# Three fp32r matmuls in place of one fp32 product in the FFT convolution of batches 2 to 8, with the rests taken by GpSimd

## The chip, the core and the metric

The kernel runs on one core of a Trainium2 chip. The metric is the device time of one execution in microseconds; the kernel before takes 2670.65 us (median of three runs, 2670.49 to 2672.26). All figures here are of that program and of one profiled execution of it.

## What is computed

Eight batches of a sequence of 3072 points with 256 channels go through a convolution by FFT and then through two dense layers:

```
X = np.fft.rfft(x, axis=1)
F = (filt_r + 1j * filt_i)[None, :, :]
y = np.fft.irfft(X * F, n=3072, axis=1)

h = np.maximum(np.maximum(x @ w1, x @ w2), x @ w3)      # 256 -> 768
x = h @ w_out                                           # 768 -> 256

h = x @ w_in                                            # 256 -> 1024
solu = h * softmax(h)
ln = (solu - mean) / sqrt(var + 1e-6) * g_ln
out = ln @ w_out                                        # 1024 -> 256
```

x is 8 x 3072 x 256 in float32. The program gets the weights as 64-bit floats and turns them to float32 itself.

## The kernel before

**Two stages.** In the first, some 1500 us, batch after batch goes through the convolution and the first dense layer ("MoE"), and its result is spilled to DRAM (lines 952 and 953). The second reads the spill and does the other layer (lines 1095 to 1200). It uses no part of what the change touches.

**Steps of the first stage.** The MoE is cut in 288 steps (b, tg, f): 8 batches, 6 tiles of 512 tokens, 6 slices of 128 of the hidden width. The text numbers them 0 to 287, so that batch b (counted from 0) begins with step 36 b and a tile with a multiple of 6. A step's `up` (line 920) is 12 matmuls of 512 columns; ScalarE, VectorE (DVE) and again both make `hm`, the maximum (925), `hh` and the rest `hl` (929). `down` (940 to 942) is 6 matmuls two steps later, with 12 more (949) at a tile's end. All operands there are split by hand in fp32r pairs, high part and rest, and each product is three matmuls: high by high, high by rest, rest by high. The PSUM pool of `h` has four banks, two steps' worth.

**The convolution.** A sequence of 3072 is 24 columns of 128 points. A chunk is one half (128 channels) of one batch, so chunk ch belongs to batch ch // 2. Chunks 0 and 1 (batch 0) are done ahead of the steps with a full complex DFT in `first_batch`. Chunks 2 to 15 are fed in by a generator, `fft_stream`, while the steps run. For each of four groups of columns a chunk does, in this order:

- `fwd_in`: twiddle factors on ScalarE and DVE into `U`, 6 x 128 columns for the three groups with `sl` other than 0;
- `middle`: two 128-point products `MA0`, `MA1` on TensorE (line 440); then `Z` (DVE, from PSUM), a swap of halves by two DMAs on SP's queue (515, 516), the filter in `M1` and `M2` (DVE), a difference on GpSimd, again a swap by DMA, and `EO` (DVE, two instructions);
- `inv_out`: two products `MB0`, `MB1` by `EO` (line 440), twiddle factors, and back into the chunk's slab `S`.

The group with `sl` 0 is treated apart and stays as it is. When both chunks of a batch are through, `inverse` combines the columns (DVE), and `flip` turns a tile for the MoE: two DVE transposes into `yt` (one for each chunk), 16 DMAs `zt<-yt` on SP's queue (line 880), then on ScalarE the cast `xh` and on DVE the rest `xl` (893, 894). The first `up` of a tile needs `xh` and `xl`. `yt` and `zt` have one buffer each.

**What sets the order.** The code after each step draws from `fft_stream` until DVE work worth 3200 ns is issued, or until 12 draws in a row brought none; `later()` makes a generator wait for the next step. The instructions so recorded are then put in order, engine by engine, by the framework's list scheduler, which goes by its own timeline and fixes each engine's queue; on the chip every engine works off its queue in that order. `have` would force convolution work out early if a tile's input were not recorded yet.

**Products.** `prod` (lines 437 to 440) is one fp32 matmul with the constant matrices `df` as stationary operand.

Of the kernel before, what the change touches and what calls it, by code (L numbers as in the profile page):

```python
# [11 lines left out]
F32R = mybir.dt.float32r  # L12
# [8 lines left out]
P = 128  # L21
# [124 lines left out]
def kernel(ctx: ExitStack, tc: tile.TileContext, x0, xr, ff, tw, dft, first_f, first_i,  # L146
# [135 lines left out]


    FULL = 2

    cost = [0.0]

# [146 lines left out]
    def rows(t, j0, j1):  # L434
        return t[:, j0:j1].rearrange("p s d -> p (s d)")

    def prod(o, mat, src, i0=None, i1=None, first=True, last=True):
        m = df[:, mat] if mat < 7 else dfull[:, mat - 7]
        v = src if i0 is None else rows(src, i0, i1)
        FZ['mm'] = nc.tensor.matmul(o, m, v, start=first, stop=last).ins  # L440

    def fwd_in(ch, g):
        sl, ks = GROUPS[g]
        X = S[ch]
        U = f2.tile([P, 8, P], F32, tag="U", name="U")
        n = len(ks)
        T = fc.tile([P, 6, P], F32, tag="T", name="T")
        if sl:
            for j, k in enumerate(ks):
                nc.scalar.activation(T[:, j:j + 4:3], X[:, sl:sl + 2, j], AF.Copy, scale=col("s", k))  # L450
                nc.scalar.activation(U[:, j:j + 4:3], X[:, sl:sl + 2, j], AF.Copy, scale=col("c", k))
            yield
            tt(U[:, 0:3], U[:, 0:3], T[:, 3:6], ALU.add)
            yield
            tt(U[:, 3:6], U[:, 3:6], T[:, 0:3], ALU.subtract)
            yield
        elif ch >= FULL:
            t, d = X[:, :, 1], X[:, :, 2]
            for j, k in enumerate((8, 20)):
                nc.scalar.activation(T[:, j], d[:, j], AF.Copy, scale=col("sh", k))  # L460
                nc.scalar.activation(U[:, j], t[:, j], AF.Copy, scale=col("c", k))
                nc.scalar.activation(T[:, 2 + j], d[:, j], AF.Copy, scale=col("ch", k))
                nc.scalar.activation(U[:, 2 + j], t[:, j], AF.Copy, scale=col("ns", k))
            yield
            tt(U[:, 0:4], U[:, 0:4], T[:, 0:4], ALU.add)
            yield
        else:
            t, d = X[:, :, 1], X[:, :, 2]
            nc.scalar.copy(U[:, 0], X[:, 0, 0])
            nc.scalar.activation(U[:, 1], X[:, 1, 0], AF.Copy, scale=col("c", 12))  # L470
            nc.scalar.activation(U[:, 5], X[:, 1, 0], AF.Copy, scale=col("ns", 12))
            nc.gpsimd.memset(U[:, 4], 0.0)
            yield
            for j, k in enumerate((8, 20)):
                nc.scalar.activation(T[:, j], d[:, j], AF.Copy, scale=col("sh", k))
                nc.scalar.activation(U[:, 2 + j], t[:, j], AF.Copy, scale=col("c", k))
                nc.scalar.activation(T[:, 2 + j], d[:, j], AF.Copy, scale=col("ch", k))
                nc.scalar.activation(U[:, 6 + j], t[:, j], AF.Copy, scale=col("ns", k))
            yield
            uu = U.rearrange("p (r s) d -> p r s d", r=2)[:, :, 2:4]  # L480
            tt(uu, uu, T[:, 0:4].rearrange("p (r s) d -> p r s d", r=2), ALU.add)
            yield
        ST["u", ch, g] = U
        yield
# [3 lines left out]
    def later():  # L488
        n = STEP[0]
        yield  # L490
        while STEP[0] == n and not NOW[0]:
            yield
# [6 lines left out]
    def middle(ch, g):  # L499
        dc = ch % 2  # L500
        sl, ks = GROUPS[g]
        n = len(ks)
        W = n * P
        real = g == 3 and ch >= FULL
        R = 2 * P if real else 0
        foff = sum(2 * P * len(GROUPS[i][1]) for i in range(4 if real else g))

        def pair(tag, name, pool=fc):
            t = pool.tile([P, 2, 4, P], F32, tag=tag, name=name)
            return t.rearrange("p r s d -> p (r s d)")[:, :2 * W].rearrange("p (r w) -> p r w", r=2)  # L510

        def swap(v):

            t = fc.tile([P, 512], F32, tag="swap", name="swap")[:, :v.free_size()]
            nc.sync.dma_start(t[64:], v[:64])
            nc.sync.dma_start(t[:64], v[64:])
            return t

        odd = ch < 2 and UNITS.index((ch, g)) % 2
        F = pair("Z" if odd else "F", "F")  # L520
        nc.sync.dma_start(F.rearrange("p r w -> p (r w)"), ff[dc, :, foff:foff + 2 * W])
        src = ST.pop(("u", ch, g))
        pf = pairbank(ch)
        if ch < FULL:
            for r, (mr, mi) in enumerate(((FRR, FIR), (FRI, FII))):
                prod(pf[:, r, :W], mr, src, 0, n, True, False)
                prod(pf[:, r, :W], mi, src, n, 2 * n, False, True)
                yield
            M1 = pair("EO", "Y", f2)
            M2 = pair("M2" if odd else "M1", "M2")  # L530
            tt(M1, pf[:, 0:1, :W].to_broadcast([P, 2, W]), F, ALU.mult)
            yield
            tt(M2, pf[:, 1:2, :W].to_broadcast([P, 2, W]), F, ALU.mult)
            yield
            tt(M1[:, 0], M1[:, 0], M2[:, 1], ALU.subtract)
            SUMS[ch, g] = tt(M1[:, 1], M1[:, 1], M2[:, 0], ALU.add).ins
            yield
            ST["y", ch, g] = M1
            yield
            return  # L540
        u = col("u", 0)
        if real:
            prod(pf[:, 0, 0:P], MO, S[ch][:, 1, 0])
            prod(pf[:, 0, P:R], MF0, S[ch][:, 0, 0])
            prod(pf[:, 0, R:W], MA0, src, 0, 2)
            yield
            prod(pf[:, 1, R:W], MA1, src, 2, 4)
            TAKEN.add(ch)
        else:
            prod(pf[:, 0, :W], MA0, src, 0, n)  # L550
            yield
            prod(pf[:, 1, :W], MA1, src, n, 2 * n)
        yield
        Z = pair("Z", "Z")
        M2 = pair("M2", "M2")
        nc.scalar.mul(M2[:, 0, R:], pf[:, 1, R:W], -1.0)
        nc.scalar.copy(M2[:, 1, R:], pf[:, 0, R:W])
        if real:
            nc.scalar.copy(Z[:, 0, :R], pf[:, 0, :R])
        stt(Z[:, :, R:], pf[:, :, R:W], u, M2[:, :, R:])  # L560
        ZS = swap(Z[:, 0])
        yield
        M1 = pair("M1", "M1")
        tt(M1[:, :, R:], Z[:, 1:2, R:].to_broadcast([P, 2, W - R]), F[:, :, R:], ALU.mult)
        if real:
            tt(M1[:, 0, :R], Z[:, 0, :R], F[:, 0, :R], ALU.mult)
        yield
        EO = pair("EO", "EO", f2)
        tt(M2[:, :, R:], ZS[:, R:].unsqueeze(1).to_broadcast([P, 2, W - R]), F[:, :, R:], ALU.mult)
        if real:  # L570
            stt(M2[:, 1, :R], ZS[:, :R], col("sg", 0), F[:, 1, :R], ALU.mult)
        yield
        tt(M1[:, 1, R:], M1[:, 1, R:], M2[:, 0, R:], ALU.subtract, nc.gpsimd)
        RS = swap(M1[:, 1, R:])
        tt(M1[:, 0, R:], M1[:, 0, R:], M2[:, 1, R:], ALU.add, nc.gpsimd)
        if real:
            tt(EO[:, 0, :R], M1[:, 0, :R], M2[:, 1, :R], ALU.add, nc.gpsimd)
        yield
        yield from later()
        with behind_step():  # L580
            stt(EO[:, 0, R:], RS, u, M1[:, 0, R:], ALU.subtract)
            stt(EO[:, 1, R:], M1[:, 0, R:], u, RS)
        yield
        ST["y", ch, g] = EO
        yield

    def inv_out(ch, g):
# [3 lines left out]
        io = 0 if sl else 1  # L591
        src = ST.pop(("y", ch, g))
        pf = pairbank(ch)
        src = src.rearrange("p r (s d) -> p (r s) d", d=P)
        if ch < FULL:
            prod(pf[:, 0, :W], IRR, src, 0, n, True, False)
            prod(pf[:, 0, :W], IIR, src, n, 2 * n, False, True)
            yield
            prod(pf[:, 1, io * P:W], IRI, src, io, n, True, False)
            prod(pf[:, 1, io * P:W], III, src, n + io, 2 * n, False, True)  # L600
        elif not sl:
            prod(pf[:, 0, :P], MOI, src, 0, 1)
            prod(pf[:, 0, P:W], MB0, src, 1, n)
            yield
            prod(pf[:, 1, 2 * P:W], MB1, src, n + 2, 2 * n)
        else:
            prod(pf[:, 0, :W], MB0, src, 0, n)
            yield
            prod(pf[:, 1, io * P:W], MB1, src, n + io, 2 * n)
        yield  # L610

        def zz(r, j):
# [146 lines left out]
    def first_batch():  # L759
# [53 lines left out]
        for i, u in enumerate(UNITS):  # L813
# [28 lines left out]
            if i == 7:  # L842
                turn_in(0, 0, *UNITS[6])
        GATE.append(behind)
        with tc.issue_after(FZ["mm"]), tc.issue_after(FZ["sent"].ins):
            for q in range(4):
                quarter(3, q, nc.scalar, xs[3, q])
# [477 lines left out]
```

## Time and profile before

| | |
|---|---|
| median of three runs | 2670.65 us |
| profiled execution, its own time | 2670.15 us |
| its span, first to last instruction | 2668.4 us |
| TensorE (PE) busy | 2648.6 us, 99% of the span |
| DVE, ScalarE (ACT), GpSimd (POOL) busy | 79%, 58%, 33% |
| line 440, PE busy | 210.5 us, all before 1340 us |
| last matmul of the first layer | about 1611 us |

The span is read by stage: what an engine has to do between 100 and 1340 us, with the convolution beside the MoE, differs from what follows. A matmul's own duration in the trace includes the time it takes to flow through the array; its price in a row of others is the distance from one start to the next. Records of one fp32 product come in pairs, so "x4" at line 440 is two products.

### The profile page before, as it was taken

What the parts mean: (1) busy time and instruction counts of PE and PEld (TensorE: products, weight loads), DVE (VectorE), ACT (ScalarE), POOL (GpSimd) and SP (SyncE); (2) the same over time, 40 slices, a digit from 0 to 9 for tenths busy, and PEclk for the clock granted to TensorE, in tenths of its full rate; (3) what the DMA queues carried; (4) which work ended last, traced back from release to release, by engine and by line L of the source; (5) the groups of instructions that cost most, each with busy time, mean ns of one, the idle gap of its engine ahead of it and who ended that gap; (6) DMA issues with size and microseconds to landing.
All of it is one profiled execution on the core that took longest, in us unless ns stands there. A gap on an engine that the chain in (4) does not pass through costs nothing.

```text
span 2668.4 us, 38588 instructions
## 1 busy us (share of the span) xinstructions
PE 2648.6 (99%) x12452; PEld 2183.5 (82%) x12452; DVE 2113.2 (79%) x3545; ACT 1559.9 (58%) x2960; POOL 892.9 (33%) x1311
## 2 busy tenths in 40 slices
PE   8999999999999999999999999999999999999999
PEld 5778888878877878888788888888888888888888
DVE  7796788987988988988785448878888878787875
ACT  5645554454454554554543336777777777777775
POOL 0011121011010010010110005666667676767675
PEclk9999999999999999999999999999999999999999
DMA  8534222224133242232222105555555555555553
GB/s 252 147 113 130 84 80 75 83 76 127 50 88 108 65 129 63 69 95 63 79 85 80 43 22 139 150 139 146 145 142 143 143 146 142 143 144 150 139 129 87
DMA packets 169063, 295.56 MB, mean 111 GB/s; under 512 B 33724, under 2 KB 101052, under 8 KB 167228
## 3 DMA queue, kind: packets, MB, share of 16 engines
q1 hardware_dynamic: 113848, 231.49, 32.4%
q10 hardware_dynamic: 53716, 56.89, 6.7%
q0 software_dynamic: 1296, 4.72, 0.6%
q8 instruction: 98, 1.61, 0.3%
q14 instruction: 105, 0.86, 0.1%
HBM read 97.40 MB, written 56.62 MB: 58 GB/s over the span
## 4 chain that ended last, share of the span: by engine, by line
PE 64%; DVE 2%; DMA 2%; SPq 1%; issue 1%; ACT 0%; POOL 0%; DVEq 0%; POOLq 0%; ACTq 0%
PE h L1111 20%; PE h L920 13%; PE p L1180 13%; PE p L1182 7%; PE o L941 2%; PE o L942 2%; PE o L940 2%; PE o L949 2%; PE pf L440 2%; SPq L880 1%; DMA swap<-M 0%; DMA swap<-Z 0%; DMA raw<-in_w_in_dram 0%; DMA raw<-in_w_out_dram 0%; DVE h L925 0%
## 5 line engine op out<-in xcount | busy, mean ns | idle before, releaser
L291 POOL TENSOR_TENSOR M<-M,M 128x384 f32<-128x384 f32 (+1 forms) x112 | 128.4, 1167 | 1093.0 <-DVE M L291 871.1
L1173 POOL TENSOR_TENSOR sl<-zt,sh 128x1024 fp32r<-128x1024 f32 x188 | 453.6, 2413 | 119.3 <-ACT sh L1172 96.7
L1180 PE MATMUL p<-V,sh 128*128 128x512 f32 x1536 | 380.4, 389 | 0.0
L928 ACT CAST hh<-h 128x512 fp32r<-128x512 f32 x288 | 169.2, 589 | 353.6 <-DVE h L925 344.5
L1122 DVE SCALAR_TENSOR_TENSOR sp<-h,e 128x1024 f32<-128x1024 f32 x192 | 234.0, 1219 | 152.6 <-ACT e L1120 150.6
L1180 PEld LDWEIGHTS p<-V,sh 128*128 128x128 f32 x1536 | 287.3, 188 | 59.3
L923 ACT ACTIVATE hm<-h 128x512 f32<-128x512 f32 x288 | 174.2, 606 | 183.5 <-PE h L920 179.0
L1120 ACT ACTIVATE e<-h,sm 128x1024 f32<-128x1024 f32 x192 | 213.8, 1114 | 110.1 <-DVE sm L1118 70.5
L1118 DVE TENSOR_REDUCE sm<-h 128x1 f32<-128x1024 f32 x192 | 231.5, 1206 | 47.0 <-PE h L1111 46.0
L1172 ACT CAST sh<-zt 128x1024 fp32r<-128x1024 f32 x188 | 196.6, 1047 | 106.6 <-PE p L1180 91.8
L1124 ACT ACTIVATE e<-sp,sm 128x1024 f32<-128x1024 f32 x192 | 220.5, 1148 | 54.2 <-DVE sm L1126 42.4
L1111 PE MATMUL h<-wih,x2h 128*128 128x512 f32 x768 | 243.1, 392 | 1.2 <-ACT xo L952 1.2
L1111 PE MATMUL h<-wih,x2l 128*128 128x512 f32 x768 | 242.0, 391 | 0.0
L925 DVE TENSOR_TENSOR h<-hm,h 128x512 f32<-128x512 f32 x288 | 196.9, 686 | 55.0 <-PE h L920 51.1
L1111 PE MATMUL h<-wil,x2h 128*128 128x512 f32 x768 | 238.3, 390 | 0.0
L1139 DVE STREAM_TRANSPOSE yt<-sp 128x1024 f32<-128x1024 f32 x188 | 231.4, 1231 | 5.3 <-DMA zt<-yt 1.5
L940 PE MATMUL o<-hh,woh 128*128 128x512 f32 x576 | 233.0, 404 | 0.0
L929 DVE TENSOR_TENSOR hl<-h,hh 128x512 fp32r<-128x512 f32 x288 | 196.0, 682 | 46.6 <-ACT hh L928 46.1
L941 PE MATMUL o<-hl,woh 128*128 128x512 f32 x576 | 228.0, 396 | 0.2 <-DVE hl L929 0.2
L942 PE MATMUL o<-hh,wol 128*128 128x512 f32 x576 | 225.8, 392 | 0.0
L1182 PEld LDWEIGHTS p<-V,sl 128*128 128x128 f32 x1536 | 209.7, 190 | 14.9
L1182 PE MATMUL p<-V,sl 128*128 128x256 f32 x1536 | 214.9, 282 | 0.0
(185 smaller groups left out, 5621.8 us busy)
## 6 DMA issues: line engine op xcount, KB each, us to landing
zt<-yt SPq DMA_DIRECT2D x752, 128.0 KB
x<-xo SPq DMA_DIRECT2D x96, 256.0 KB
x<-x ACTq DMA_DIRECT2D x48, 512.0 KB
F<-in_ff_dram SPq DMA_DIRECT2D x48, 384.0 KB
S<-in_xr_dram SPq DMA_DIRECT2D x12, 1536.0 KB
out_dram<-ob ACTq DMA_DIRECT2D x144, 128.0 KB
zt<-yt SPq DMA_DIRECT2D x560, 32.0 KB
F<-in_ff_dram SPq DMA_DIRECT2D x16, 512.0 KB
```

What stands on the lines that cost most here:

```text
L920: nc.tensor.matmul(ph[j], wt[:, c, f * P:(f + 1) * P], xt[:, c], start=i == 0, stop=i == 5)
L940: nc.tensor.matmul(po[m], wo_h[:, f, cs], hh, start=f == 0, stop=False)
L941: nc.tensor.matmul(po[m], wo_h[:, f, cs], hl, start=False, stop=False)
L942: nc.tensor.matmul(po[m], wo_l[:, f, cs], hh, start=False, stop=False)
L1111: nc.tensor.matmul(h[:, fs], xt[:, c, ts], wt[:, c, fs], start=n == 0, stop=n == 5)
L1118: nc.vector.tensor_reduce(sm[:, 0:1], h, axis=AX.X, op=ALU.max, negate=True)
L1122: nc.vector.scalar_tensor_tensor(sp, h, 1.0, e, op0=ALU.mult, op1=ALU.mult, accum_out=sm[:, 2:3])
L1124: nc.scalar.activation(e, sp, AF.Square, bias=sm[:, 3:4], accum_out=sm[:, 4:5])
L1139: nc.vector.transpose(out=YT[g][:, :, t].rearrange("p j c k -> p c j k"), in_=sp.rearrange("p (c j k) -> p c j k", c=NF2, j=4))
L1173: nc.gpsimd.tensor_tensor(lv, z, hv, op=ALU.subtract)
L1180: nc.tensor.matmul(p, sh[:, c], V2[:, c], start=c == 0, stop=False)
L1182: nc.tensor.matmul(p[:, :D], sl[:, c], V2[:, c, :D], start=False, stop=c == NF2 - 1)
```

## The change

Where a chunk is 2 to 15 and the group's `sl` is not 0, `U` and `EO` (128 x 768 each) are split before the products: ScalarE casts the high part to fp32r, GpSimd subtracts it for the rest. `prod` then makes three fp32r matmuls of 384 columns with the constants `dh` and `dl`, split once at the end of `first_batch` into the buffer of `dfull`. Both splits are followed by a `later()`. There are 14 chunks x 3 groups = 42 pairs of splits (84 casts, 84 subtractions) and 42 x 4 = 168 products, which become 504 matmuls. The four new tiles `Uh`, `Ul`, `EOh` and `EOl` take 3 KB a partition each, and the scratch of the software DMA queue is 4 KB a partition in place of 16. One product of `inv_out` is written in another way, with the same columns.

```
+    SPLIT = tuple(range(2, 16))
+    def split(v, tag):
+        hi, lo = (fc.tile([P, 6, P], F32R, tag=tag + s, name=tag + s) for s in "hl")
+        nc.scalar.copy(hi, v)
+        nc.gpsimd.tensor_tensor(lo, v, hi, op=ALU.subtract)
+        return hi, lo
...
     def prod(o, mat, src, i0=None, i1=None, first=True, last=True):
+        if isinstance(src, tuple):
+            hi, lo = (rows(v, i0, i1) for v in src)
+            dh, dl = FZ["dh"][:, mat], FZ["dl"][:, mat]
+            nc.tensor.matmul(o, dh, hi, start=True, stop=False)
+            nc.tensor.matmul(o, dl, hi, start=False, stop=False)
+            nc.tensor.matmul(o, dh, lo, start=False, stop=True)
+            return
...
+            if ch in SPLIT:
+                U = split(U[:, :6], "U")
+                yield
+                yield from later()
...
+        if sl and ch in SPLIT:
+            EO = split(EO.rearrange("p r (s d) -> p (r s) d", d=P), "EO")
+            yield
+            yield from later()
...
+        if SPLIT:
+            dd = fc.tile([P, 2, 4, P], F32R, tag="dfull", name="dd")
+            FZ["dh"], FZ["dl"] = dd[:, 0], dd[:, 1]
+            with tc.issue_after(FZ["sent"].ins):
+                nc.scalar.copy(FZ["dh"], df[:, 0:4])
+            nc.gpsimd.tensor_tensor(FZ["dl"], df[:, 0:4], FZ["dh"], op=ALU.subtract)
...
-    nc = bacc.Bacc("TRN2", target_bir_lowering=False, num_devices=1)
+    nc = bacc.Bacc("TRN2", target_bir_lowering=False, num_devices=1, dynamic_dma_scratch_size=4096)
```

The edit moves every later line by 8 to 30, so 440 becomes 449 to 451 (the three matmuls), 880 becomes 910, 920 becomes 950, 925 and 929 become 955 and 959. It also moves the instructions in the queues. Counted by the rows of line 929 (959) that stand ahead of it, the last product of chunk 15 stands in step 232 before and in step 246 after, and the second transpose of the first tile of batches 2 to 7 stands at steps 53, 101, 132, 168, 204 and 239 before, and at 59, 95, 134, 174, 214 and 249 after, where the tiles' first `up` is step 78 (their second tile, since the first goes another way), 108, 144, 180, 216 and 252.

**PE, step 200 before and step 216 after.** `pf` is a PSUM bank of a product, `EO` its moving operand (`EOh` and `EOl` the new pair), `dd` the new constants, `o` the sum of `down`.

```order
L920 MATMUL h_10859<-xl_10634,w0h_138 128x512 x2
L920 MATMUL h_10859<-xh_10633,w0l_140 128x512 x2
L440 MATMUL pf_10216<-EO_10093,df_136 128x384 x2
L941 MATMUL o_10792<-hl_10789,woh_145 128x512
L942 MATMUL o_10792<-hh_10788,wol_146 128x512
```

```order
L449 MATMUL pf_10877<-EOh_10823,dd_661 128x384
L450 MATMUL pf_10877<-EOh_10823,dd_661 128x384
L451 MATMUL pf_10877<-EOl_10824,dd_661 128x384
L449 MATMUL pf_11056<-Uh_10904,dd_661 128x384
L450 MATMUL pf_11056<-Uh_10904,dd_661 128x384
L451 MATMUL pf_11056<-Ul_10905,dd_661 128x384
L950 MATMUL h_12174<-xh_12091,w0h_138 128x512
L950 MATMUL h_12175<-xh_12091,w1h_139 128x512
```

Where two fp32 matmuls stood between those of a step, two times three stand now; at step 216 they come behind all of tile (5,5) and ahead of the first `up` of batch 6, whose two `h` banks then alternate.

**DVE, the transposes for the first tile of batch 6** (`yt`; `S` is a chunk's slab), before and then after.

```order
L929 TENSOR_TENSOR hl_10877<-h_10860,hh_10876 128x512
L925 TENSOR_TENSOR h_10887<-hm_10900,h_10887 128x512
L876 STREAM_TRANSPOSE yt_11275<-S_7601 128x4x4x32
L876 STREAM_TRANSPOSE yt_11275<-S_9246 128x4x4x32
L929 TENSOR_TENSOR hl_10904<-h_10887,hh_10903 128x512
```

```order
L303 SCALAR_TENSOR_TENSOR S_9777<-scr_10749 128x2x384 x2
L955 TENSOR_TENSOR h_12065<-hm_12078,h_12065 128x512
L906 STREAM_TRANSPOSE yt_11876<-S_9777 128x4x4x32
L955 TENSOR_TENSOR h_12106<-hm_12119,h_12106 128x512
L303 SCALAR_TENSOR_TENSOR Z_10889<-pf_10873,tws_135,M2_10890 128x768
L303 SCALAR_TENSOR_TENSOR EO_10751<-swap_10756,tws_135,M1_10680 128x384
L303 SCALAR_TENSOR_TENSOR EO_10751<-M1_10680,tws_135,swap_10756 128x384
L959 TENSOR_TENSOR hl_12082<-h_12065,hh_12081 128x512
L959 TENSOR_TENSOR hl_12123<-h_12106,hh_12122 128x512
L299 TENSOR_TENSOR M1_10908<-Z_10889,F_10871 128x768
L299 TENSOR_TENSOR M2_10890<-swap_10894,F_10871 128x768
```

The two transposes stood together in step 204; the second now follows the maximum of step 214 (`h_12065`), right behind the last instruction of `inverse`, and the maximum of step 215 (`h_12106`) follows it.

**SP, the 16 DMAs of that tile**, before and then after (`swap` are the swaps of halves, `F` a filter load).

```order
L880 DMA zt_11276<-yt_11275 32x256 x7
L515 DMA swap_10496<-Z_10490 64x512
L516 DMA swap_10496<-Z_10490 64x512
L880 DMA zt_11276<-yt_11275 32x256 x4
L515 DMA swap_10513<-M1_10506 64x256
L516 DMA swap_10513<-M1_10506 64x256
L521 DMA F_11108<-in_ff_dram 128x768
L880 DMA zt_11276<-yt_11275 32x256 x5
```

```order
L910 DMA zt_11877<-yt_11876 32x256 x4
L534 DMA swap_10894<-Z_10889 64x384
L535 DMA swap_10894<-Z_10889 64x384
L910 DMA zt_11877<-yt_11876 32x256 x4
L540 DMA F_11054<-in_ff_dram 128x768
L534 DMA swap_10942<-M1_10908 64x384
L535 DMA swap_10942<-M1_10908 64x384
L910 DMA zt_11877<-yt_11876 32x256 x8
```

Both orders have swaps among the 16; after, the last eight stand behind a swap of `M1_10908`, which is made from the `Z_10889` that follows the maximum of step 215.

## Rows read from the trace of the kernel before

**Rows 1.** The page's first part; 210 to 1110 us, busy by engine; a PE wait.

```profile
PE 2648.6 (99%) x12452; PEld 2183.5 (82%) x12452; DVE 2113.2 (79%) x3545; ACT 1559.9 (58%) x2960; POOL 892.9 (33%) x1311
...
210.00:1110.00 900.00, 899.46 (x3972) 725.40 (x3971) 776.00 (x1195) 463.40 (x1058) 100.72 (x90) 1.00 0.29 87
...
PE pf L440 <- DVE EO L295: 0.3, 1, 0.3
```

**Rows 2.** Timeline of PE, first stage: start, duration, line, operands, count.

```profile
705.51 1.45 PE L440 MATMUL pf<-U,df 128*128 128x384 f32 x4
706.50 0.92 PE L920 MATMUL h<-xh,w1h 128*128 128x512 f32 x2
707.26 0.63 PE L920 MATMUL h<-xl,w1h 128*128 128x512 f32 x2
```

**Rows 3.** Timeline of PE, second stage: eight matmuls of 512 columns, eight of 256.

```profile
2004.18 1.98 PE L1180 MATMUL p<-V,sh 128*128 128x512 f32 x8
2006.00 1.11 PE L1182 MATMUL p<-V,sl 128*128 128x256 f32 x8
2006.95 0.63 PE L1111 MATMUL h<-wih,x2h 128*128 128x512 f32 x2
```

**Rows 4.** Groups by tile: min/median/max ns, first and last start.

```profile
L619 ACT COPY v<-pf x12: 778/800/802, 34.4 to 238.7; 128x768 f32<-128x768 f32 x12
L1061 POOL TENSOR_TENSOR wil<-we,wih x4: 1289/1301/1317, 1371.9 to 1385.5; 128x512 fp32r<-128x512 f32 x4
L291 POOL TENSOR_TENSOR EO<-M,M x14: 722/740/1507, 180.6 to 1330.1; 128x256 f32<-128x256 f32 x14
```

**Rows 5.** Groups by line and shape: count, busy us, mean ns, idle before.

```profile
L295 DVE SCALAR_TENSOR_TENSOR Z<-pf,tws,M 128x768 f32<-128x768 f32 x42 | 42.3, 1008 | 9.2 <-ACT M L557 9.0
L291 DVE TENSOR_TENSOR M<-swap,F 128x768 f32<-128x768 f32 x42 | 39.8, 948 | 10.2 <-DMA swap<-Z 10.2
L295 DVE SCALAR_TENSOR_TENSOR EO<-M,tws,swap 128x384 f32<-128x384 f32 x42 | 25.6, 610 | 0.0
L929 DVE TENSOR_TENSOR hl<-h,hh 128x512 fp32r<-128x512 f32 x288 | 196.0, 682 | 46.6 <-ACT hh L928 46.1
L893 ACT CAST xh<-zt 128x512 fp32r<-128x512 f32 x70 | 40.8, 642 | 0.0
L876 DVE STREAM_TRANSPOSE yt<-S 128x512 f32<-128x512 f32 x70 | 45.6, 685 | 11.8 <-DMA zt<-yt 11.6 <-issue 0.2
L291 DVE TENSOR_TENSOR scr<-scr 128x384 f32<-128x384 f32 x46 | 27.0, 626 | 0.0
L291 DVE TENSOR_TENSOR S<-scr 128x768 f32<-128x768 f32 x34 | 31.8, 962 | 0.0
L295 DVE SCALAR_TENSOR_TENSOR S<-scr 128x768 f32<-128x768 f32 x46 | 41.6, 944 | 0.0
```

**Rows 6.** Timelines of SP's queue and DVE: a tile's 16 DMAs, a swap's two.

```profile
1417.82 11.17 SPq L880 DMA_DIRECT2D zt<-yt  x16
1430.40 1.31 DVE L876 STREAM_TRANSPOSE yt<-S 128x512 f32<-128x512 f32 x2 [4.92 <-DMA zt<-yt]
...
956.52 0.46 SPq L515 DMA_DIRECT2D swap<-M  x1
957.03 0.60 SPq L516 DMA_DIRECT2D swap<-M  x1
```

**Rows 7.** Timeline of PE, then windows of PE: length, busy, granted clock, DMA.

```profile
90.79 5.30 PE L865 MATMUL h<-im,z 96*128 96x96 f32 x24 [2.46 <-ACT S L796]
...
91.00:92.00 1.00, 1.00 (x6) 0.51 1.14 204
...
101.00:102.00 1.00, 1.00 (x5) 0.87 0.07 25
```

**Rows 8.** Timelines of DVE and GpSimd: one instruction, and two, that took long.

```profile
1103.06 1.77 DVE L295 SCALAR_TENSOR_TENSOR scr<-scr,S 128x768 f32<-128x768 f32 x1
...
910.84 4.32 POOL L291 TENSOR_TENSOR M<-M,M 128x384 f32<-128x384 f32 x2 [73.22 <-DVE M L291]
```

More of the change, by code (lines that the diff above doesn't have):

```diff
@@ L593, in inv_out @@
         pf = pairbank(ch)
-        src = src.rearrange("p r (s d) -> p (r s) d", d=P)
+        if not isinstance(src, tuple):
+            src = src.rearrange("p r (s d) -> p (r s) d", d=P)
         if ch < FULL:
@@ L608, in inv_out @@
             yield
-            prod(pf[:, 1, io * P:W], MB1, src, n + io, 2 * n)
+            prod(pf[:, 1, :W], MB1, src, n, 2 * n)
         yield
```

## The prediction

> **What bounds the kernel now.** I read the busy times first: TensorE is busy for 99% of the span, and in 210 to 1110 us, where the changed work lies, for 899.46 of 900 us, against 776 of DVE, 463 of ScalarE and 101 of GpSimd [rows 1]. The waits of PE come next: on the products' operand `EO` it waited once, 0.3 us [rows 1]. So TensorE's own work sets the time there, and a microsecond taken from it is won, as long as the operands still come in time. The third look is at prices of TensorE's work [rows 2, 3], the fourth at what must be done between a chunk's last columns and the next batch's first `up` [rows 5, 6], the fifth at the clock behind a wait [rows 7].
>
> **Part 1, the products: -21.5 us.** From 705.51 to 707.26 there are 1.75 us, in which two fp32 products of 384 columns and two fp32r matmuls of 512 start [rows 2]. Eight fp32r matmuls of 512 take 2006.00 - 2004.18 = 1.82, or 0.2275 each, and eight of 256 take 0.95, or 0.119 each [rows 3]. So a product costs (1.75 - 2 x 0.2275)/2 = 0.648. An fp32r matmul of 384 columns stands midway between 0.119 and 0.2275, at 0.173, and three cost 0.520. That is 0.128 less, and 168 x 0.128 = 21.5 us. Bounds: 0.16 for the matmul, in proportion to the columns alone, would be 28; with 0.19, if every change of weights costs a little more, it would be 13.
>
> **Part 2, the splits: nothing on ScalarE and GpSimd by their sums, but a latency.** A ScalarE copy of 128x768 takes 0.80 [rows 4], so 84 casts are 67 us over some 1100, on an engine that is half idle [rows 1]. A GpSimd subtraction takes 0.74 at 256 columns and 1.30 at 512 [rows 4]; along that line 768 cost 1.86, and 84 make 156 us, on an engine with 800 of 900 us free [rows 1]. If the other work were not there, each pair would cost TensorE its 2.7 us; it is there, since `later()` puts the products behind the next step, which is 18 matmuls of 0.2275, 4.1 us. What remains is that a product's operand comes 2.7 us later, in a queue that had 0.3 us of waits. I take 3.0 us for waits on `U` and `EO` outside the two places of part 4, between 0 and 6: the lower end is what the 0.3 of [rows 1] says, the upper a wait of 2 us at three of the 84 splits, and I take the middle.
>
> **Part 3, constants and scratch: +0.6 us.** The high part of the constants is a cast of 512 columns, 0.64 by the row of `xh` [rows 5], at the end of `first_batch`, where ScalarE's copies of `S` are already what TensorE waits for [rows 7]. I count it whole, 0.6 (0 to 1.3, the upper end if the subtraction is waited for too). The subtraction, 1.30 [rows 4], stands on GpSimd between weight DMAs and is needed by the first split product, many steps later. The smaller scratch I put at nothing: the software queue moves 1296 packets in all in the profiled execution, nine DMAs' worth, none of them beside the steps that count here. If it did bind, one weight would come later in the first 100 us.
>
> **Part 4, the end of a batch: +14.2 us.** Here the gain can go. The `later()`s make chunks end later. The second transpose for batch 6 moves from step 204 to 214, with the first `up` at 216; that for batch 7 from 239 to 249, with the first `up` at 252. Before, 12 steps, some 50 us, lay between; now one or two. I add up step 216 in the order of the rows on SP and DVE that the section on the change shows, from the end of the `up` of step 215, t = 0. The maximum of 215 ends at about 1.1 (0.7 as its like `hl`, and some 0.4 before it starts). Then `Z` 1.01, to 2.1; two `EO` of 0.61, to 3.3; two `hl` of 0.68, to 4.6; `M1` and `M2`, 0.95 each, to 6.5 [rows 5]. GpSimd's difference of 384 columns takes 1.0 on the line of part 2, to 7.5. The swap's two DMAs hold SP for 0.46 and 0.60 [rows 6], to 8.5. Only then come the last eight of the 16 `zt` DMAs, 0.70 each (16 in 11.17 [rows 6]), to 14.1. Landing takes 1430.40 - 1417.82 - 11.17 = 1.4 [rows 6], to 15.5, and the cast `xh` 0.64 [rows 5], to 16.2.
>
> Against this TensorE has, ahead of that `up`, the 18 `down` matmuls of the steps left and the tile's 12 more, 30 x 0.2275 = 6.8, and 12 matmuls of 384, 2.1; in between it waits for `EOh` (`EO` at 3.3, cast to 4.1, while TensorE is there after 13 matmuls at 3.0), 1.2. It is through at 10.1 and stands for 6.1, which with the 1.2 is **7.3 us** (3 if the DMAs are already issued ahead of the swap on the chip, 10 if DVE is behind by a chunk).
>
> For step 252, from the end of the `up` of 249: DVE still has the last combinations, 2 x 0.63 + 2 x 0.96 + 0.68 + 2 x 0.94 = 5.7 [rows 5], less what is done by then; I put the maximum of 249 at 4.2 and the transpose at 4.9. All 16 DMAs follow, 11.2, to 16.1; with landing and cast the operand is there at 18.1. TensorE has 72 matmuls, 16.4. It waits **1.8 us** (0 to 5).
>
> **The clock.** At 90.79 TensorE had waited 2.46 us; from 91 on the granted clock is 0.51 of 2.4 GHz, the lower level of 1.2, and between 101 and 102 it is back on average at 0.87 [rows 7]. So some 10.2 us were run at half speed, and 5.1 lost. The wait at 216 is longer than that one, so I add **5.1 us** once; the 1.8 at 252 is shorter, and I add none. Sum of the part: 7.3 + 5.1 + 1.8 = 14.2.
>
> **Sum.** -21.5 + 3.0 + 0.6 + 14.2 = -3.7 us on the profiled execution's 2670.15: 2666.45. The median of the runs is 0.5 above that execution, so 2667.0. A difference of 0.2%, 5.3 us, is about what can be told from no change: faster is below 2665.3, slower above 2676.0.
>
> **Rivals.**
>
> *No wait at the batches' ends: 2653.* If DVE and SP reach the transposes and DMAs of step 216 earlier against TensorE than my sum has it, only parts 1 to 3 are left: 2670.65 - 21.5 + 3.6 = 2652.8; with a wait shorter than the 2.46 of the row, which leaves the clock up, as much as 2655, and with half the part-2 waits too, 2651. For it: the order before has the same pattern (the `up` of two steps alternating behind a finished tile) at four other steps (30, 36, 54 and 60, within 210 to 1110 us), and the 900 us hold 0.54 us of idle time in all [rows 1]. Against it: the sum needs 6 us to be wrong by. Chance 0.28.
>
> *The clock falls three times: 2678.* The wait at 252 reaches 2.5 us (0.7 more than I have), the clock falls there too (5.1), and one of the waits of part 2 also reaches 2.5 (5.1): -3.7 + 0.7 + 10.2 = +7.2, so 2677.9. Its place is TensorE in front of the first `up` of batch 7 and in front of a product by `EOh`. It turns into slower only with the third fall. For it: the price of a wait is more than its length [rows 7], and 18.1 against 16.4 is a close race. Against it: ordinary products have 2.7 us of new latency in 4.1 of cover. Chance 0.20.
>
> *GpSimd holds up DVE: 2673.* In the trace a DVE instruction of 768 columns with two operands took 1.77 where its like takes 0.95, and a pair of GpSimd subtractions of 384 took 4.32 in place of 2.0 [rows 5, 8]: when both run, one stands. The change adds some 62 GpSimd subtractions of 1.86 us in 210 to 1110 (84 over about 1220 us). If each kept DVE for its whole length, it would be 62 x 1.86 = 115 us of DVE; the 900 us, less the 15.9 that TensorE would win there (62/84 of 21.5), leave 884.1 - 776 = 108. DVE would then be 7 us over, and with the ends of batches -3.7 + 7 = +3, near 2673. The Trainium skill, page "SBUF — State Buffer", section "SBUF: two separate sides", states such a rule: a DVE instruction with two SBUF inputs and a GpSimd one that reads SBUF take the shared port in turns, each for the whole instruction. The two rows of group 8 agree with it in kind; that every subtraction should meet one is what no row here bears out. Against the rival: DVE spends much of its time on instructions that read PSUM, and the 900 us hold 90 GpSimd instructions already with TensorE at 99.9%. Chance 0.06.
>
> *The products are not cheaper: 2688.* If a 384-column fp32r matmul cost 0.216, three would cost what the fp32 product does, and the waits alone would be left: 2667.0 + 21.5. The 256-column row at 0.119 speaks against it. Chance 0.04.
>
> **How the numbers follow.** My forecast, 2667.0, holds 0.42 (2661 to 2673 by itself, 0.16 of it below 2665.3). Faster: 0.28 + 0.16 = 0.44. Same: 0.26 + 0.06 = 0.32. Slower: 0.20 + 0.04 = 0.24. The range goes from 2652, the case without waits, to 2679, the case of three falls with its rounding; beyond it lie the last rival, a third of the case of three falls and the lower tail, about 0.18.
>
> **What the profile of after would show.** Part 1: eight starts of the matmuls at 449 to 451 in a row spaced by some 0.17 us, and 21 us less of TensorE work. Part 2: TensorE's waits on `Uh`, `Ul`, `EOh`, `EOl` adding to about 3 us. Part 3: a wait ahead of the first steps longer by up to 0.6. Part 4: a wait of some 6 us ahead of line 950 at the first `up` of batch 6, put down to `xh`, with windows of granted clock 0.5 for ten us behind it, and a short one for batch 7 without. DVE instructions stretched beside GpSimd's would speak for the fourth case. I am wrong if the wait at step 216 is not there (then the time is near 2653), or if the clock falls at more places than one.

## The result: 2705 us, 1.3% slower

The changed kernel takes 2705.31 us (median of four runs, 2703.43 to 2709.34), against 2670.57 for the kernel before in the same comparison: a ratio of 1.0128, with a 95% interval of 1.0116 to 1.0141. The prediction was 2667.0, with a range that ended at 2679. The profiled execution has a span of 2707.6 us, 39.2 more than the 2668.4 of before.

The first part of the page after, which answers to the first of [rows 1]:

```profile
PE 2648.6 (98%) x12620; PEld 2215.9 (82%) x12620; DVE 2167.6 (80%) x3545; ACT 1621.1 (60%) x3045; POOL 1066.8 (39%) x1396
```

Three things stand in it. ScalarE has 61 us more (1621.1 - 1559.9) and GpSimd 174 more, which are the casts and subtractions (67 and 156 were counted). But DVE, to which the change gives **nothing** (3545 instructions in both), is busy 54.4 us longer. And PE's busy time has not fallen: some of its work now runs at the lower clock.

Where PE stood: its waits by line and releaser (us in total, times, longest).

```profile
PE o L971 <- DVE hl L959: 18.8, 11, 4.3
PE o L970 <- ACT hh L958: 9.0, 2, 4.6
PE pf L455 <- DVE Y L299: 6.5, 5, 2.1
PE h L950 <- ACT hm L953: 4.2, 6, 1.4
PE pf L449 <- ACT S L675: 4.2, 2, 3.6
...
PE h L950 <- ACT xh L923: 1.7, 1, 1.7
...
PE pf L451 <- POOL Ul L291: 0.2, 1, 0.2
```

All lines of this view add up to 54.9 us, against 15.7 before. The long ones are waits of `down` for `hl` and `hh`, the MoE's own operands, which the change does not touch. The new operands are hardly waited for: 0.2 us for `Ul`, and none for `EOl`. (Of the 4.2 us at line 449, 3.65 stand in front of a product by `Uh`, but end with ScalarE's `S<-pf`, which reads an earlier product's result from PSUM.)

The clock is the third part. Summed over windows of 2 us, one less the granted clock gives the time lost: 5.1 us before, all of it behind the wait at 90.79 of [rows 7], and 23.9 after. The windows of PE at one of the places (length, then busy and count of PE, PEld, DVE, ACT, POOL, then granted clock, DMA share, GB/s):

```profile
1266.00:1272.00 6.00, 2.22 (x10) 1.42 (x8) 6.00 (x7) 0.94 (x4) 5.20 (x3) 1.00 0.36 101
1272.00:1274.00 2.00, 0.80 (x1) 0.29 (x1) 2.00 (x4) 1.07 (x3) 0.00 (x0) 0.59 0.14 33
1274.00:1276.00 2.00, 1.15 (x3) 0.95 (x4) 2.00 (x4) 0.83 (x1) 0.86 (x1) 0.50 0.35 82
1276.00:1278.00 2.00, 2.00 (x7) 1.61 (x6) 2.00 (x2) 0.00 (x0) 0.97 (x1) 0.50 0.36 87
```

PE waits 4.41 us up to 1272.63, and behind that the clock stands at half. There are five such falls after 150 us, with the waits that end at 358.77 (3.14 us), 858.12 (4.58), 1060.61 (4.28), 1272.63 (4.41) and 1287.09 (3.65). They cost 15.4 us, 1.7 to 3.4 each. The rest of the 23.9 is the fall behind the wait of [rows 7], which the kernel before has too, and two short ones at 29.93 and 53.82, ahead of the first instruction of the change.

So the balance is: -21.5 for the products, +39.2 of waits (54.9 - 15.7), +18.8 of clock (23.9 - 5.1), together +36.5, against +39.2 measured. The terms overlap a little: 3.1 of the clock's microseconds lie within PE's own waits, where half speed costs nothing, so that the sum is nearer +33.

**The saving is real.** PE's timeline after, on the two split products of a chunk (start, duration, line):

```profile
843.43 0.34 PE L450 MATMUL pf<-Uh,dd 128*128 128x384 f32 x1
843.60 0.34 PE L451 MATMUL pf<-Ul,dd 128*128 128x384 f32 x1
843.79 0.34 PE L449 MATMUL pf<-Uh,dd 128*128 128x384 f32 x1
843.96 0.34 PE L450 MATMUL pf<-Uh,dd 128*128 128x384 f32 x1
844.13 0.34 PE L451 MATMUL pf<-Ul,dd 128*128 128x384 f32 x1
844.31 0.63 PE L950 MATMUL h<-xl,w1h 128*128 128x512 f32 x2
```

Five starts in 844.31 - 843.43 = 0.88 us are 0.176 each. The prediction had 0.173, from [rows 3].

**What a long wait is made of.** The wait of 4.58 us at 858.12 is read from four engines. PE first, then GpSimd, ScalarE and DVE in the ten us ahead of it:

```profile
852.93 0.61 PE L950 MATMUL h<-xh,w1l 128*128 128x512 f32 x2
858.12 0.80 PE L970 MATMUL o<-hh,woh 128*128 128x512 f32 x1 [4.58 <-ACT hh L958]
...
847.68 7.10 POOL L291 TENSOR_TENSOR Ul<-U,Uh 128x768 fp32r<-128x768 f32 x1 [7.20 <-ACT Uh L290]
854.75 1.94 POOL L299 TENSOR_TENSOR M<-M,M 128x384 f32<-128x384 f32 x2
...
856.72 0.49 ACT L575 ACTIVATE M<-pf 128x384 f32<-128x384 f32 x1 [8.67 <-POOL M L299]
857.11 0.47 ACT L576 COPY M<-pf 128x384 f32<-128x384 f32 x1
857.47 1.09 ACT L958 CAST hh<-h 128x512 fp32r<-128x512 f32 x2
...
850.10 0.68 DVE L924 TENSOR_TENSOR xl<-zt,xh 128x512 fp32r<-128x512 f32 x1
850.70 1.81 DVE L303 SCALAR_TENSOR_TENSOR S<-scr 128x768 f32<-128x768 f32 x2
852.44 0.68 DVE L924 TENSOR_TENSOR xl<-zt,xh 128x512 fp32r<-128x512 f32 x1
853.04 0.68 DVE L955 TENSOR_TENSOR h<-hm,h 128x512 f32<-128x512 f32 x1
```

From the bottom up: DVE runs instruction after instruction with two operands in SBUF (the last combinations of a batch and `xl`), until at 853.04 the maximum comes, which reads PSUM. The subtraction `Ul`, started at 847.68, takes 7.10 us. Its median is 1.85, and 854.78 - 1.85 = 852.93, which is just where DVE's row of such instructions ends: it seems to have stood until then. Behind it in GpSimd's queue stand the two differences `M<-M,M` of the chunk; behind those, on ScalarE, a copy `M<-pf` into the same buffer, which waits 8.67 us; and behind that copy, in ScalarE's queue, the two casts `hh`. PE waits for `hh`. Nothing in this chain is an operand that the change added.

In other places DVE is the one that stands. Before the wait at 358.77:

```profile
353.97 3.33 POOL L299 TENSOR_TENSOR M<-M,M 128x384 f32<-128x384 f32 x2 [2.70 <-DVE M L299]
...
353.81 0.95 DVE L299 TENSOR_TENSOR S<-scr 128x768 f32<-128x768 f32 x1
354.68 3.44 DVE L303 SCALAR_TENSOR_TENSOR S<-scr 128x768 f32<-128x768 f32 x2
358.04 0.68 DVE L959 TENSOR_TENSOR hl<-h,hh 128x512 fp32r<-128x512 f32 x1
```

Two `S<-scr` took 1.81 above and 3.44 here, beside GpSimd's differences; `hl`, for which PE waits, stands right behind.

### The profile page after: what moved, and what is told of

Read it like the earlier page. It is cut to its first block, busy times and chain, and to the rows that moved or that the text cites. A ratio compares the mean times of both kernels' runs of the same rounds, so it can differ in the third digit from the quotient of the medians.

```text
span 2707.6 us, 39121 instructions
## 1 busy us (share of the span) xinstructions
PE 2648.6 (98%) x12620; PEld 2215.9 (82%) x12620; DVE 2167.6 (80%) x3545; ACT 1621.1 (60%) x3045; POOL 1066.8 (39%) x1396
## 4 chain that ended last, share of the span: by engine, by line
PE 60%; DVE 6%; issue 1%; DMA 1%; SPq 1%; ACT 1%; POOL 0%; DVEq 0%; ACTq 0%; POOLq 0%
PE h L1141 19%; PE p L1210 13%; PE h L950 12%; PE p L1212 7%; PE o L979 2%; PE o L971 2%; PE o L972 2%; PE o L970 2%; DVE scr L299 2%; DVE S L299 1%; DMA swap<-M 1%; DVE h L955 1%; DVE hl L959 1%; DVE S L303 1%; SPq L910 0%
## 5 line engine op out<-in xcount | busy, mean ns | idle before, releaser
L291 POOL TENSOR_TENSOR Ul<-U,Uh 128x768 fp32r<-128x768 f32 x42 | 94.2, 2243 | 530.5 <-ACT Uh L290 502.0
L971 PE MATMUL o<-hl,woh 128*128 128x512 f32 x576 | 228.8, 397 | 20.0 <-DVE hl L959 18.8
L299 POOL TENSOR_TENSOR M<-M,M 128x384 f32<-128x384 f32 (+1 forms) x112 | 119.6, 1088 | 252.7 <-DVE M L299 203.4
```

The costliest lines, as they stand in the source:

```text
L971: nc.tensor.matmul(po[m], wo_h[:, f, cs], hl, start=False, stop=False)
```

## The experiments

Each ratio is against runs of the kernel before that were made beside the run in question; their medians lie between 2670.6 and 2674.0 us.

Theory A at the outset: GpSimd's new subtractions and DVE hold each other up. Rival B: the two `later()` put the work into a worse order. Rival C: the 84 casts on ScalarE stand ahead of `hm` and `hh`.

**Rests on DVE.**

```
-        nc.gpsimd.tensor_tensor(lo, v, hi, op=ALU.subtract)
+        nc.vector.tensor_tensor(lo, v, hi, op=ALU.subtract)
```

> The changed kernel with the rests of the splits subtracted by DVE in place of GpSimd; all else as in it. Theory A (GpSimd's long subtractions and DVE's two-operand instructions hold each other up, so that DVE and, through GpSimd's queue, ScalarE come late, and PE waits for hl, hh): no stretched DVE instruction beside GpSimd is left, but DVE gets 84 x 0.95 = 80 us of honest work, more than the some 50 us by which it is stretched now; waits of PE stay, fewer or of another kind: 2660 to 2695. Theory B (the two later() put the chunks' work in a worse order, whoever does the rests): waits as now, 2700 to 2710. Theory C (ScalarE's 84 casts stand ahead of hm and hh): 2700 to 2710.

Measured: 2687.62 us, a ratio of 1.006 (1.0045 to 1.0075), as A had it, and against B and C. What is left of the loss stands at two places, as PE's timeline shows (only rows with a wait above 2.3 us):

```profile
1059.26 0.44 PE L449 MATMUL pf<-Uh,dd 128*128 128x384 f32 x1 [2.38 <-ACT S L675]
1063.80 0.66 PE L449 MATMUL pf<-EOh,dd 128*128 128x384 f32 x1 [3.21 <-DVE Z L303]
1068.78 1.22 PE L455 MATMUL pf<-S,df 128*128 128x128 f32 x4 [2.44 <-ACT S L675]
...
1250.12 0.79 PE L970 MATMUL o<-hh,woh 128*128 128x512 f32 x1 [2.81 <-ACT hh L958]
1253.55 0.80 PE L971 MATMUL o<-hl,woh 128*128 128x512 f32 x1 [2.63 <-DVE hl L959]
1263.41 0.44 PE L449 MATMUL pf<-Uh,dd 128*128 128x384 f32 x1 [2.39 <-ACT S L675]
1267.95 0.80 PE L950 MATMUL h<-xh,w0h 128*128 128x512 f32 x1 [3.21 <-ACT xh L923]
```

These are steps 180 and 216, the first `up` of batches 5 and 6. There the second transposes stand in steps 180 and 215 in this kernel's order, so the batches end late, as the prediction's part 4 described for step 216. That the lateness makes these waits, and not DVE's 84 added rests at the same place, is argued from the place and not shown.

**No rests, and memsets in their place.**

```
-        nc.gpsimd.tensor_tensor(lo, v, hi, op=ALU.subtract)
-        return hi, lo
+        return hi, hi
...
-            nc.tensor.matmul(o, dh, lo, start=False, stop=True)
+            nc.tensor.matmul(o, dl, lo, start=False, stop=True)
```

> The changed kernel without the subtractions: no rest of U and EO is made, and the third matmul takes the rest of the constants by the high part a second time, so TensorE's work is the same (the part of the result that the operand's rest brings is left out). The casts and both later() stay. Theory A (GpSimd's subtractions): most waits go, the saving of the products shows, 2645 to 2665. Theory B (order by later()): 2695 to 2710. Theory C (casts on ScalarE): 2695 to 2710.

```
+        nc.gpsimd.memset(v, 0.0)
+        nc.gpsimd.memset(v, 0.0)
+        nc.gpsimd.memset(v[:, :3], 0.0)
```

> As the run without rests (third matmul with the constants' rest by the high part; the operand's rest is left out), but GpSimd overwrites each split operand with zeros behind its cast, in three instructions of 768, 768 and 384 columns, some 2.0 us by the 0.21 of a memset of 128 and the 0.10 of one of 1 column. So GpSimd waits for the same cast, is busy about as long and holds the same buffer, but reads no operand. Theory A-port (two instructions with operands in SBUF hold each other up): DVE is not stretched and the time is that of the run without rests, 2655 to 2667. Theory A-queue (GpSimd's queue is too long, its differences and what waits for them come late): 2685 to 2710.

Measured: 2659.08 us (ratio 0.9957, 0.9943 to 0.9971) and 2659.46 (0.9947, 0.9932 to 0.9962). Each memset of 768 columns took 0.74 and that of 384 took 0.42, so GpSimd was busy 1.90 us a split, as with the subtraction, and no time went. Casts, `later()`s and GpSimd's queue are all there, and the saving shows: B, C and A-queue fall for this order. The order is not quite that of the changed kernel, though: the second transposes of batches 6 and 7 stand in steps 210 and 247, or 209 and 245, instead of 214 and 249.

**No later().** Both `yield from later()` behind the splits are taken out.

> The changed kernel without the two later() behind the splits; casts, subtractions and matmuls stay. Theory B (order by later()): the waits go, 2645 to 2665. Theory A (GpSimd's subtractions): the waits on hl and hh stay, and waits on the operands' rests may come to them, 2695 to 2725. Theory C (casts): 2695 to 2710.

Measured: 2712.74 us (1.0163, 1.0147 to 1.0178), within A's range. B falls. The second transposes stand in 214 and 249 here too, without the `later()`s: what makes the chunks late in the scheduler's order is the splits in the chain, not `later()`.

**Splits that nobody uses, with subtractions and with memsets.** The products are fp32 as before, and no `later()` follows:

```
-                U = split(U[:, :6], "U")
+                split(U[:, :6], "U")
...
-            EO = split(EO.rearrange("p r (s d) -> p (r s) d", d=P), "EO")
+            split(EO.rearrange("p r (s d) -> p (r s) d", d=P), "EO")
```

> The products are fp32 as before; the splits (casts on ScalarE, subtractions on GpSimd) and the constants' split are made and used by nobody, with no later() behind them. TensorE's work is that of the kernel before. Theory A: PE waits of some 20 to 40 us come back though nobody uses the rests, 2685 to 2715. Theory B: as the kernel before, 2668 to 2674. Theory C: 2680 to 2710 too, but with waits behind casts and none behind stretched DVE instructions or GpSimd.

> The run with unused splits (fp32 products, nobody reads the splits, no later()), with GpSimd's subtractions replaced by three memsets of the high part (768, 768 and 384 columns, 1.9 us by the runs with memsets). The order of the second transposes is that of the kernel before, 203 or 204 and 239, in both runs of the pair, so the order is out of the comparison. If GpSimd's reading beside DVE is the cause of the 52 us that the unused splits cost: 2668 to 2680. If it is the length of GpSimd's queue, or the casts on ScalarE: 2700 to 2725.

Measured: 2722.82 us (1.02, 1.0184 to 1.0217) with the subtractions and 2685.77 (1.0051, 1.0038 to 1.0064) with memsets. In both the second transposes stand as in the kernel before, so the order of the batches' ends is out of it. The unused splits cost 52 us, more than A's range, and 39 of these go when GpSimd only writes. The other 13 us fit neither range of the second expectation: they belong to the casts, to GpSimd's occupied queue or to details of the order, and these runs do not part them. Groups of DVE by form show what reading does (count, busy us and mean ns, idle before), `M<-Z,F` in the kernel before, then `M<-Z,F` and `M<-swap,F` in the changed kernel, then with unused subtractions, then with unused memsets, then with the rests on DVE:

```profile
L291 DVE TENSOR_TENSOR M<-Z,F 128x768 f32<-128x768 f32 x42 | 39.8, 947 | 0.3
```

```profile
L299 DVE TENSOR_TENSOR M<-Z,F 128x768 f32<-128x768 f32 x42 | 49.7, 1183 | 0.3
L299 DVE TENSOR_TENSOR M<-swap,F 128x768 f32<-128x768 f32 x42 | 44.0, 1049 | 11.7 <-DMA swap<-Z 11.7
```

```profile
L299 DVE TENSOR_TENSOR M<-Z,F 128x768 f32<-128x768 f32 x42 | 49.4, 1175 | 0.3
L299 DVE TENSOR_TENSOR M<-swap,F 128x768 f32<-128x768 f32 x42 | 50.3, 1198 | 11.2 <-DMA swap<-Z 11.0
```

```profile
L301 DVE TENSOR_TENSOR M<-Z,F 128x768 f32<-128x768 f32 x42 | 40.0, 952 | 0.3
L301 DVE TENSOR_TENSOR M<-swap,F 128x768 f32<-128x768 f32 x42 | 40.2, 956 | 17.7 <-DMA swap<-Z 17.7
```

```profile
L299 DVE TENSOR_TENSOR M<-Z,F 128x768 f32<-128x768 f32 x42 | 39.7, 946 | 0.2
L299 DVE TENSOR_TENSOR M<-swap,F 128x768 f32<-128x768 f32 x42 | 39.9, 949 | 10.3 <-DMA swap<-Z 9.9
```

The same instruction takes 946 to 956 ns on average, as in [rows 5], in the runs in which GpSimd has no rests to take, and 1175 to 1198 (1049 in one case) in the two shown here in which it takes all 84. DVE's whole busy time says the same for its 3545 instructions: 2113.2 us before, 2167.6 in the changed kernel, 2185.3 with unused subtractions, 2116.5 with unused memsets.

**Which of the splits.** `EO` alone, `U` alone, and `EO` with `U` of the third group alone, all with rests on GpSimd:

> The changed kernel with EO alone split (84 of the 168 products as three fp32r matmuls, 42 casts, 42 subtractions on GpSimd with their later()); U's products stay fp32. The saving is half, 10.7 us. Theory A1 (what hurts is the subtractions of U beside the last combinations of a batch, where DVE is full: the Ul took up to 7.10 us there): waits mostly gone, 2660 to 2668. Theory A2 (every subtraction on GpSimd hurts alike): half of the loss and half of the gain, 2682 to 2692.

> The changed kernel with U alone split (the other 84 products). Theory A1: nearly all waits stay and half the saving goes, 2698 to 2712. Theory A2: 2682 to 2692.

> EO split in all three groups, U in the third alone, rests on GpSimd: the changed kernel without the 28 splits of U in the two groups that run beside the last combinations of a batch. Saving 112 x 0.128 = 14.3 us. Theory A1 (it is those 28 splits that hurt): 2658 to 2675, near EO alone. Theory A2 (all 84 alike): two thirds of the loss of 56 us, 37, less 14: 2688 to 2698.

Measured: 2673.98 us (1.0000, 0.999 to 1.0009), 2700.68 (1.0095, 1.0079 to 1.0111) and 2686.75 (1.0051, 1.0034 to 1.0067). `EO`'s rests do little harm: the time is at neither range but that of before. Their 10.7 us of saving are eaten by 7.9 us of more waits, all short. `U`'s do much: the time is in A1's range. But A1, that only the 28 splits of `U` beside the last combinations hurt, falls too: the 14 of the third group cost 13 us over `EO` alone, though they save 3.6. DVE's busy time is 2127.2, 2145.8 and 2140.4 us.

The two kinds of rests stretch different instructions. With `EO` alone it is the chunk's own `M<-Z,F`, nearly as much as in the changed kernel, and yet the time is that of before:

```profile
L299 DVE TENSOR_TENSOR M<-Z,F 128x768 f32<-128x768 f32 x42 | 48.6, 1156 | 0.2
```

With `U` alone `M<-Z,F` is at 948 ns, and the sums of `inverse` grow (`scr<-scr,S` of 768 columns, 22 of them: 949 ns before, 950 with `EO` alone, 1152 with `U` alone), at the ends of batches, where DVE has no slack.

**Mixed engines.** Three more versions move the rests, or some of them, to DVE: `EO` and `U` of the third group on DVE; `EO` on GpSimd with `U` of the third group, or all of `U`, on DVE.

> EO split in all three groups, U in the third alone (112 of 168 products, 14.3 us of saving), and the 56 rests by DVE in place of GpSimd, 53 us of DVE work, none of it on U of the two groups that run beside the last combinations. If theory A and the place (A1) hold, the waits stay short: 2658 to 2666. If 53 us more on DVE are too many wherever they are: 2670 to 2685.

> EO split in three groups with the rests on GpSimd, U in the third group alone with the rests on DVE. From the runs so far: EO's rests on GpSimd cost about 8 us of small waits against 10.7 saved, U's rest on GpSimd in the third group about 16; on DVE it should cost 14 x 0.95 = 13 us of DVE work and little of PE's. Theory A (what hurts is GpSimd reading while DVE has U, inverse work and hm's maxima queued): 2662 to 2670. If any rest beside U costs its time wherever it is done: 2676 to 2690.

> All 84 splits as in the changed kernel, the rests of EO on GpSimd, those of U on DVE (42 x 0.95 = 40 us). Theory A with DVE's own load as the second limit (the run with all rests on DVE was at 2688): the DVE work beside the last combinations still gets 28 rests, 27 us, so waits stay there: 2668 to 2682. If only GpSimd's reading hurts: 2652 to 2662.

Measured: 2671.72 us (0.9998, 0.9987 to 1.001), 2677.93 (1.0014, 1.0006 to 1.0023) and 2697.67 (1.009, 1.0074 to 1.0105). The first two are in the dearer of their ranges: a rest costs something wherever it is done. The last misses both of its ranges: with `EO`'s rests on GpSimd it is some 8 us over the run with all rests on DVE (1.009 against 1.006), which has the second transposes in the same steps (180, 215, 248). Here too DVE and GpSimd read side by side, but why it costs that much when `EO` alone costs little is not settled.

**Fewer chunks, rests on DVE.**

```
-    SPLIT = tuple(range(2, 16))
+    SPLIT = tuple(range(2, 10))
```

and the same with `range(2, 8)`.

> Rests on DVE, all splits, in chunks 2 to 9 alone (96 of 168 products, 12.3 us of saving, 48 rests). With all chunks split and rests on DVE the waits, some 25 us, and the clock falls, 15 us, all stood at two ends of batches (steps 180 and 216), where the second transposes stood at 180 and 215; here they stand at 173 and 211. If the lateness of a batch's end is the second cause: no such wait, 2658 to 2665. If DVE's added work costs time wherever it is: 2670 to 2680.

> The same in chunks 2 to 7 alone (72 products, 9.2 us of saving, 36 rests); the second transposes stand at 167, 205 and 240, as in the kernel before (168, 204, 239). Lateness as the second cause: 2661 to 2666. DVE's added work: 2668 to 2676.

Measured: 2668.22 us (0.9984, 0.9975 to 0.9993) and 2670.61 (0.9995, 0.9985 to 1.0005). Both lie above the range that lateness alone would give, the second in that of DVE's added work. The waits at the two ends are gone, and after 150 us the clock no longer falls. That fits lateness as the cause but does not part it from the load: chunks 10 to 13, which run up to these two ends, have no casts and no rests here either. Short waits, mostly for `hm`, come with ScalarE's and DVE's added work and take back half of the saving. With chunks 2 to 9 the kernel is the only one here with rests that is measurably faster than before, by 0.16%.

**The scratch alone.**

> The kernel before with the software queue's scratch at 4 KB in place of 16, and nothing else. If the scratch costs nothing: within 2668 to 2673. If its 9 DMAs wait for room: 2675 or more, with longer waits in the first 150 us.

Measured: 2672.69 us against 2673.38 (0.9998, 0.9988 to 1.0007). No cost shows.

The balance of the profiled executions, in us against the kernel before: the products' saving by the prediction's price, more waits of PE (sum of that view), more time lost to the clock, and the span:

| run | saving | waits | clock | sum | span |
|---|---|---|---|---|---|
| changed kernel | -21.5 | +39.2 | +18.8 | +36.5 | +39.2 |
| rests on DVE | -21.5 | +23.3 | +15.4 | +17.2 | +13.7 |
| no rests | -21.5 | +8.4 | 0 | -13.1 | -13.6 |
| memsets | -21.5 | +6.7 | +3.4 | -11.4 | -11.6 |
| no later() | -21.5 | +46.1 | +6.8 | +31.4 | +42.0 |
| unused, subtractions | 0 | +35.1 | +5.1 | +40.2 | +53.1 |
| unused, memsets | 0 | +9.3 | +3.4 | +12.7 | +17.5 |
| `EO` alone | -10.7 | +7.9 | 0 | -2.8 | -1.3 |
| `U` alone | -10.7 | +28.8 | +6.8 | +24.9 | +30.6 |
| DVE, chunks 2 to 9 | -12.3 | +6.6 | -1.7 | -7.4 | -5.2 |

The clock's column also counts half speed while PE waits anyway: 3.1 us in the changed kernel, 6.4 with the rests on DVE, under 1 in the others. Less that, the sum with the price of 0.128 us a product comes within 3 us of the span in five runs. It leaves 5 to 7 us in three (the changed kernel, unused memsets, `U` alone), and 12 and 14 in two (no `later()`, unused subtractions), which the records of waits don't name.

## Why the prediction was wrong

**Part 1, the products, held.** 0.176 us a matmul against 0.173; the two runs without GpSimd's reading come to -13.6 and -11.6 with their waits named. Of part 3's 0.6 nothing shows: the wait of 2.46 us at 90.79 is one of 2.22 after, and the scratch alone has no cost.

**Part 2 failed, and it is the step that decided.** "Nothing on ScalarE and GpSimd by their sums" counted each engine's time by itself: 1.86 us a subtraction was right (the median is 1.85, the mean 2.11), but it is also paid by DVE, 54.4 us in all, and by whoever stands behind GpSimd. The term put at nothing cost, by the pair of runs with unused splits, 39 us. I put 3.0 us of waits on `U` and `EO`, and looked for them at the new operands. These are waited for 0.2 us. The waits came at `hl`, `hh` and `hm`, 32 us against 2.5 before, on DVE and ScalarE, beside and behind which the new work runs.

**The rival "GpSimd holds up DVE" was the mechanism, at a chance of 0.06 and with the wrong size.** It had DVE held up for 115 us, twice the 54.4 measured, and priced that by an average over 900 us, in which DVE falls only 7 us short. But DVE has no slack at all where a batch ends. The windows of the kernel before say so, in the same columns as above:

```profile
650.00:700.00 50.00, 50.00 (x222) 41.31 (x221) 49.90 (x77) 20.51 (x45) 0.00 (x0) 1.00 0.15 43
850.00:900.00 50.00, 49.93 (x219) 40.72 (x218) 49.93 (x73) 21.53 (x43) 0.00 (x0) 1.00 0.13 39
1050.00:1100.00 50.00, 50.00 (x220) 40.88 (x219) 50.00 (x72) 25.64 (x54) 0.00 (x0) 1.00 0.16 46
```

DVE is busy for all but 0.1 of 50 us there, and GpSimd does **nothing** (x0). So the trace of before held no price for GpSimd's work in the one stretch in which it is dear, and the 776 of 900 in [rows 1] hid that. The rival also priced one direction only: DVE standing for GpSimd. The other, GpSimd standing for DVE with ScalarE's queue behind it, makes the longest wait (4.58 us). Ahead of the 4.41 there is both: `Ul` takes 3.89 us, the two differences behind it 3.39, and beside these two `S<-scr` on DVE take 3.68. The Trainium skill, page "SBUF — State Buffer", section "SBUF: two separate sides", says that a DVE instruction with two SBUF inputs and a GpSimd one that reads SBUF take a shared port in turns. The runs agree in kind: with a GpSimd that only writes, 1.90 us a split, `M<-Z,F` is back at 952 ns; and the 7.10 us of `Ul` end 1.74 us after DVE turns to an instruction that reads PSUM.

**Part 4 was right in kind, wrong in its cause, and partly in its places.** The wait for `xh` at step 252 measured 1.68 us, against 1.8, but that is luck. The sum had the 16 DMAs come too late. They came in time: the next transposes, which wait for them, start at 1468.66, before PE is through.

```profile
1468.66 1.30 DVE L906 STREAM_TRANSPOSE yt<-S 128x512 f32<-128x512 f32 x2 [2.40 <-DMA zt<-yt]
1469.37 1.07 ACT L982 COPY xo<-o 128x512 f32<-128x512 f32 x2 [1.06 <-PE o L979]
1470.33 1.15 ACT L923 CAST xh<-zt 128x512 fp32r<-128x512 f32 x2
1471.01 0.50 PE L950 MATMUL h<-xh,w0h 128*128 128x512 f32 x1 [1.68 <-ACT xh L923]
```

The cast `xh` stands in ScalarE's queue behind two copies `xo`, which wait for PE's own last matmuls (line 979); these copies and the cast are the 1.68 us. At step 216 there was none for `xh`; there were 4.41 and 1.42 us at the `down` of step 214 and 3.65 at a product by `Uh`, with two falls of the clock where one was counted. The run with the rests on DVE has the late ends without GpSimd's share (and with 84 rests more on DVE): waits and clock of two places make up its whole loss. But the lateness is not `later()`'s doing, as the run without them shows.

**The clock.** "Three falls" was the condition of the slower rival; there were five after 150 us. They cost 15.4 us, 3.1 each on average, where the sum took 5.1 for one. I had it decide by the third fall and gave it 0.20, since I saw only two places where a wait could get long enough.

**The forecast's sign** rested on [rows 8] being a rarity. There, 126 GpSimd subtractions (112 `M<-M,M` and 14 `EO<-M,M`) lay beside DVE's work; the change adds 84 that are nearly twice as long, and puts them where DVE is full.

## What to carry to other kernels

Work on an engine that is idle by its sum is free only if it shares nothing with the engine that is full: ask what the two read from, and look at windows in which the *other* engine is at 100%, since an average over the stage hides them. A group of unchanged instructions whose mean grows, here 947 to 1183 ns, is the mark of it in the trace. The mark tells that the two meet, not what it costs: with `EO` alone the mean is 1156 ns and the time that of before. And to tell a shared port from a long queue, replace the work by some of the same length that reads nothing.

## What the hardware did that I had not expected

A GpSimd subtraction of 1.85 us took 7.10 beside DVE, nearly four times its length. And the clock did not go by the length of one wait alone: behind PE's wait of 2.43 us at 355.00 in the run without rests it stayed at 1.00, while in the run with unused memsets it fell to 0.50 behind one of 2.30 us, at 340.15.
